# A gated recurrence and a gated feed-forward block on one core: transposes of q and k moved from the DMA crossbar to TensorE, and slab groups 4, 4, 4, 4, 4, 2, 2 with a new order

## The chip, the cores and the metric

The kernel runs on one core of a Trainium2 chip. The metric is the device time of one execution in microseconds (us); lower is better. An execution's time holds the span (first to last instruction) and a little more around it.

The engines are PE (TensorE, matrix products; PEld are its weight loads), DVE (VectorE), ACT (ScalarE, which has to load a table when it changes between some functions), POOL (GpSimd) and SP (SyncE, which here only issues DMAs). Each engine works through its own queue in the order in which instructions were put there. 16 DMA engines move the data.

## The reference

```python
B, H, S, D = 4, 8, 768, 48
mag = sqrt(a_re**2 + a_im**2)
scale = minimum(mag, 0.999) / (mag + 1e-6)
a_re_n, a_im_n = a_re * scale, a_im * scale
for t in range(S):                       # per batch and head; state is D x D, complex
    new_re = ar * S_re - ai * S_im       # ar, ai: row t of a_re_n, a_im_n
    new_im = ar * S_im + ai * S_re
    S_re, S_im = new_re + outer(k[t], v[t]), new_im
    y[t] = q[t] @ S_re
x = y, heads joined: (B * S, 384)
gate = sigmoid(x @ w_gate)               # 384 -> 1536
out = (gate * (x @ w_val)) @ w_out       # 1536 -> 384, fp32, (3072, 384)
```

## The kernel before

The sequence is cut into 6 chunks of 128 rows. A *slab* is one chunk of one batch with all heads, 128 rows x 384 columns; there are 24, in the order chunk 0 of batches 0 to 3, chunk 1 of batches 0 to 3, and so on. Slab m belongs to batch m % 4. `SIZES` puts neighbouring slabs into groups; some steps are done once for a group (logarithms, the exponential of them, the arctangent), the others once for a slab or a pair.

The recurrence of a chunk is made parallel by writing the decay as a magnitude and an angle and summing both over the rows.

- `lr`, `la` load the two parts of a for a slab, `sq` and `add` make the squared magnitude, `lna`, `lnm`, `inv`, `r`, `atan` turn it into log magnitude and angle for the whole group. `lh`, `ll`, `th`, `tl` split them into two fp16 parts; `SPLIT` says in which groups.
- `cl` sums the log magnitudes over the rows by a matmul with a triangular matrix (fp32 in the first four slabs, two fp16 matmuls in the others), `ee` takes the exponentials exp(+) and exp(-), `qke` multiplies q and k with them (`lk`, `lq`, `lv` load k, q, v; `v16` makes v fp16).
- `ct` sums the angles, `r16` and `nid` bring them into one turn, `cr` carries the last row to the next chunk, `ab` and `cs` make cosine and sine. `qs` multiplies q and k by both and writes the *slot* of the slab: for each head 128 columns (cosine and sine parts, with a gap of zeros), for q and for k.
- q and k must then lie with the rows of the slab along the free axis. Slabs in `CROSSED` (6 to 23) do it by DMA: `xk` and `xq` are one transposing DMA each (line 871), issued on SP's queue, from the slot into a tile `qkT`. The others (0 to 5) do it on PE: `tp` transposes the eight 128x128 blocks of four heads into one PSUM bank (lines 892 and 893), and `qkT` copies the bank to the tile (the helper of lines 517 to 521, on DVE or ACT). There are two such halves in a slab.
- `sc` makes the scores k x q, four heads to a bank, `mst` applies the triangular mask on DVE. `kv` and `P` add the chunk's k x v to the batch's state; `u` and `x16` decay the state by the factor of the chunk and make it fp16. `y` adds masked scores x v and q x state; `y16`, `xp`, `xt` scale and transpose the result for the feed-forward block.
- The feed-forward block works on pairs of slabs. `pg` and `pv` (line 1043) are the gate and value products, 72 steps of each, 6 matmuls to a step, `tanh` on ACT gives the gate, `p` on DVE multiplies (line 1061), `po` (line 1082) multiplies by w_out in three steps for each slab, `ot` copies the bank out and `st` stores it. `wg`, `wv`, `wo` load the weights on POOL's queue.

All steps are recorded in a plan, and the order in which they are put into the queues is written out by hand: `TIMES` has a due time for each step of each kind, and steps are issued in the order of these times. So a step's place in every queue follows from its due time, SP's loads, stores and transposing DMAs too. `HOME` says by a letter for each slab or pair which engine does a step (v DVE, a ACT, g POOL). `SLOTS` gives the buffer of each tile, and of each PSUM bank under "ps" (8 banks). `WARM` puts dummy matmuls of 128 columns ahead of a step on PE (line 1131). Table loads for ACT are put where the order needs them (line 1125).

Of the kernel before, what the change touches and what calls it, by code (L numbers as in the profile page):

```python
# [27 lines left out]
CROSSED = range(6, 24)  # L28
# [3 lines left out]
SPLIT = range(2, 8)  # L32
MSTP = ()
HOME = {
    "sq": "vagvaaggaagagagaaggagggg",
    "add": "vvvvgggggggggggggggggggg",
    "lh": "gvggggvggggg",
    "r": "vvgggggggggg",
    "v16": "vavagaggggagggggagavaaga",
    "qke": "vvvggggvggggggggggggvggg",  # L40
    "th": "aagvaagvgaav",
    "ab": "vvavvavaavaaaaaaaaaavaaa",
    "qkT": "vavavvvvavvvvvvvvvvvvvvvvvvvvvvvvvvvvvvvvvvvvvvv",
    "P": "vava",
    "u": "ggggggvggggggggggvgg",
    "x16": "ggaavgaggggvggag",
    "y16": "avvvaavvavavvvavaaavaaaa",
    "xt": "vvvvvvavvvvvavvavvvvvaav",
    "ot": "vvvvvaaavvvvavvaaavvaaavv",
}  # L50
SIZES = [2, 2, 4, 4, 4, 4, 2, 2]
TIMES = {
    "wg": [
        27.89, 36.02, 27.27],
    "wv": [
        31.35, 38.17, 36.03],
    "wo": [
        53.47, 54.3, 65.03],
    "lr": [
        0.75, 2.68, 7.03, 7.06, 24.34, 27.88, 25.83, 26.32, 45.89, 58.15,  # L60
        53.31, 52.18, 71.46, 92.9, 87.25, 85.33, 106.38, 121.07, 118.57,
        112.93, 170.37, 176.96, 133.38, 160.02],
    "la": [
        2.22, 1.85, 10.78, 7.07, 24.5, 26.36, 25.84, 27.87, 48.76, 56.39,
        53.93, 53.32, 75.86, 92.85, 87.77, 85.34, 111.4, 121.08, 121.86,
        118.56, 176.57, 178.21, 153.22, 134.91],
    "sq": [
        7.04, 7.02, 11.86, 9.9, 24.95, 29.54, 26.34, 29.5, 49.21, 58.89,
        56.85, 62.71, 83.72, 96.51, 92.96, 86.01, 112.9, 129.56, 128.24,
        118.61, 180.83, 185.55, 167.29, 170.36],  # L70
    "add": [
        7.05, 7.9, 13.4, 13.88, 26.35, 38.15, 28.5, 38.12, 53.3, 65, 62,
        65.86, 87.2, 96.54, 96.47, 92.92, 121.81, 129.58, 128.25, 129.55,
        184.23, 185.57, 169.56, 170.39],
    "lna": [
        9.92, 14.99, 33.31, 67.86, 98.47, 139.01, 185.56, 171.42],
    "lh": [
        8.54, 14.47, 40.53, 42.65, 69.29, 75.89, 102.61, 103.34, 136.22,
        141.84, 185.59, 172.91],
    "lnm": [  # L80
        11.87, 15.39, 38.16, 66.46, 100.65, 132.15, 185.58, 170.4],
    "inv": [
        9.93, 16.37, 36.01, 70.07, 103.36, 139.02, 186.18, 172.85],
    "r": [
        10.77, 19.16, 40.52, 39.65, 73.59, 75.88, 108.19, 107.9, 142.65,
        142.64, 189.11, 173.82],
    "cl": [
        14.97, 14.96, 17.84, 16.27, 45.44, 42.85, 47.17, 46.54, 70.89, 76.95,
        80.11, 77.54, 104.14, 104.52, 114.2, 116.75, 138.97, 140.17, 148.32,
        149.93, 187.16, 186.78, 181.01, 173.23],  # L90
    "ee": [
        16.91, 14.98, 18.49, 17.83, 47.18, 44.65, 48.42, 47.56, 72.96, 79.27,
        86.25, 79.29, 106.53, 106.39, 114.78, 117.62, 140.01, 141.81, 149.19,
        152.85, 189.76, 189.77, 182.5, 173.81],
    "scr": [
        35.3, 38.13, 41.19, 37.26, 52.64, 53.49, 54.34, 53.48, 87.94, 92.86,
        95.76, 92.91, 118.58, 111.43, 121.83, 124.54, 153.21, 155.22, 160.22,
        160.21, 195.89, 195.1, 187.57, 187.58],
    "rbt": [
        46.92, 48.74, 55.48, 96.46, 126.03, 161.47, 198.36, 188.29],  # L100
    "arr": [
        50.09, 50.04, 55.92, 98.24, 127.86, 161.92, 205.03, 188.88],
    "lk": [
        16.93, 15.41, 15.42, 17.85, 30.76, 49.23, 53.94, 66.48, 75.91, 85.35,
        94.86, 88.08, 112.25, 92.84, 112.27, 118.55, 125.19, 156.21, 161.95,
        146.39, 185.54, 190.51, 161.93, 181.02],
    "lq": [
        16.94, 16.28, 16.95, 21.91, 41.18, 50.73, 62.72, 69.68, 79.24, 92.87,
        95.78, 88.09, 112.26, 104.92, 122.21, 118.59, 155.19, 156.9, 161.96,
        146.4, 190.31, 197.73, 161.94, 190.12],  # L110
    "lv": [
        15.4, 29.55, 9.91, 26.79, 30.86, 50.74, 71.28, 66.47, 52.19, 92.94,
        76.96, 95.79, 133.17, 121.82, 125.2, 146.64, 160.01, 154.52, 171.41,
        166.24, 140.93, 180.62, 192.37, 195.11],
    "v16": [
        15.89, 30.3, 14.95, 27.29, 45.52, 60.69, 71.29, 84.58, 87.19, 101.96,
        114.07, 118.91, 136.26, 130.58, 142.92, 147.37, 164.44, 155.21,
        178.63, 169.53, 167.28, 202.72, 198.62, 205.05],
    "qke": [
        17.82, 16.36, 20.04, 24.35, 48.73, 53.28, 67.87, 71.45, 84.59, 93.48,  # L120
        96.49, 92.93, 112.96, 108.55, 134.93, 121.8, 157.53, 160.03, 167.43,
        157.52, 209.72, 205.09, 191.58, 190.32],
    "atan": [
        14.48, 21.92, 40.57, 75.9, 108.2, 143.28, 191.6, 176.95],
    "ct": [
        15.44, 15.43, 22.66, 24.05, 48.2, 49.65, 58.14, 59.2, 83.81, 87.93,
        91.11, 87.21, 116.85, 121.09, 130.19, 122.59, 151.79, 158.27, 164.99,
        155.16, 205.89, 202.2, 191.28, 189.92],
    "r16": [
        15.45, 18.69, 23.57, 25.71, 49.24, 50.7, 58.9, 59.78, 84.57, 89.07,  # L130
        91.94, 87.95, 117.61, 121.2, 132.12, 123.7, 152.84, 159.36, 165.57,
        156.87, 207.37, 204.03, 192.35, 190.49],
    "nid": [
        16.92, 19.28, 24.33, 26.3, 49.49, 52.17, 59.3, 60.37, 85.16, 89.47,
        92.89, 88.87, 118.54, 121.4, 132.33, 124.35, 153.03, 160, 166.46,
        157.5, 208.97, 205.07, 192.97, 191.11],
    "cr": [
        20.92, 23.58, 25.85, 28.76, 50.72, 53.37, 62.74, 64.56, 87.18, 91,
        95.81, 89.85, 119.29, 122.19, 134.27, 126.29, 156.88, 161.48, 167.96,
        157.86],  # L140
    "ab": [
        17.28, 20.91, 26.31, 26.78, 52.62, 53.29, 60.7, 63.2, 87.24, 91.46,
        95.8, 89.46, 118.9, 122.61, 134.26, 126.3, 155.17, 162.17, 167.97,
        158.26, 209.12, 205.47, 195.76, 192.33],
    "cs": [
        21, 23.59, 26.51, 30.73, 52.63, 54.33, 65.04, 65.87, 88.07, 92.06,
        98.25, 91.47, 121.01, 124.52, 134.92, 126.94, 156.89, 162.18, 170.33,
        160.19, 209.71, 205.48, 195.77, 192.34],
    "qs": [
        21.9, 24.04, 29.56, 33.52, 54.31, 56.84, 67.89, 72.97, 89.48, 94.21,  # L150
        98.26, 92.95, 122.6, 125.18, 136.25, 128.26, 157.55, 163.7, 175.58,
        160.2, 210.61, 207.38, 198.38, 192.88],
    "tp": [
        24.94, 24.49, 26.86, 25.82, 30.88, 33.51, 34.4, 34.25, 56.38, 61.19,
        63.19, 59.9],
    "qkT": [
        26.18, 26.33, 27.86, 28.51, 34.86, 34.87, 38.11, 38.14, 59.65, 61.99,
        63.91, 61.2],
    "sc": [
        30.87, 26.8, 29.51, 30.31, 36, 35.29, 39.63, 38.75, 63.38, 62.7,  # L160
        64.55, 65.43, 76.51, 76.73, 80.49, 79.88, 99.76, 98.23, 103.88,
        103.37, 108.76, 108.54, 110.29, 105.52, 133.14, 130.57, 133.37,
        132.11, 144.9, 144.91, 141.57, 146.38, 167.92, 166.23, 170.32, 170.09,
        182.04, 182.27, 179.73, 179.08, 219.4, 218.3, 218.53, 215.46, 205.46,
        204.01, 202.19, 202.47],
    "mst": [
        30.89, 27.26, 31.34, 30.74, 37.25, 35.55, 40.05, 39.66, 64.58, 63.18,
        64.99, 65.85, 79.26, 77.55, 82.04, 82.03, 102, 99.99, 104.53, 103.57,
        110.54, 110.53, 114.09, 106.37, 133.57, 132.13, 134.9, 133.19, 145.74,
        145.73, 144.93, 148.33, 168.49, 167.42, 171.45, 170.52, 184.25,  # L170
        183.56, 182.51, 181.03, 220.93, 221.67, 220.95, 217.02, 205.91,
        204.43, 204.02, 204.04],
    "kv": [
        30.75, 40.06, 77.33, 35.62, 84.19, 72.09, 98.02, 90.24, 111.38,
        111.17, 121.02, 125.17, 144.87, 141.37, 152.83, 166.03, 180.81,
        171.19, 180.6, 186.17],
    "P": [
        39.64, 45.46, 79.28, 40.54, 87.17, 75.87, 101.65, 90.99, 112.95,
        112.94, 121.1, 127.85, 144.94, 142.63, 153.44, 168.15, 183.57, 186.38,
        181.05, 192.36],  # L180
    "y": [
        31.46, 33.3, 37.89, 42.66, 67.91, 67.88, 87.23, 85.97, 102.59, 105.07,
        116.74, 121.03, 136.85, 137.26, 146.6, 148.7, 171.4, 171.84, 186.37,
        183.14, 221.99, 221.25, 207.36, 205.1],
    "y16": [
        34.24, 34.88, 38.76, 42.68, 69.67, 69.27, 88.11, 86.71, 103.55,
        105.77, 116.76, 121.13, 138.98, 139, 148.73, 149.96, 172.01, 172.45,
        187.59, 187.81, 222.6, 222.41, 207.97, 205.88],
    "xp": [
# [201 lines left out]
def kernel(  # L391
# [165 lines left out]

    for g, n in enumerate(SIZES):
        m0 = FIRST[g]
# [602 lines left out]
```

## Time and profile before

| | us |
|---|---|
| median of 3 runs (lowest, highest) | 247.29 (247.19, 247.33) |
| the profiled execution's own time | 246.99 |
| its span | 244.9 |
| PE busy | 215.4 |
| DVE busy | 206.3 |
| ACT busy | 198.6 |
| POOL busy | 145.9 |

The profile is one execution with the time of every instruction. Busy times are sums over the whole span, and stages differ in what limits them; matmuls are pipelined, so that a busy PE is not PE at its peak. A line of a group gives line, engine, operation, output and inputs, shape and count, then the busy time in us and the mean of one instruction in ns, then the idle time just before them and what ended it. Of the DMA queues, SP's moved 37.80 MB in 166800 packets (loads, stores and transposing DMAs), the one of POOL 3.57 MB.

### The profile page before, as it was taken

The page shows a single profiled execution, that of the slowest core. Times are in us where ns is not written, and L with a number is a line of the kernel's source. Part 1 is how long each engine was busy: PE and PEld are TensorE (multiplying, and loading weights), DVE is VectorE, ACT ScalarE, POOL GpSimd, SP SyncE. Part 2 cuts the span into 40 slices and gives each one's busy share as a digit, 9 for nine tenths or more (in the row PEclk, how much of TensorE's full clock was granted, in tenths as well). Part 3 has the DMA queues.
Part 4 walks back from the last instruction along what each step waited for, and adds up shares of the span by engine and source line. Part 5 has one row for each costly group of instructions (what it writes and reads, how often), then busy time and mean ns, then how long its engine had stood idle before and what let it go on. Part 6 is the DMA issues. An engine that isn't in the chain of part 4 may idle for free.

```text
span 244.9 us, 6068 instructions
## 1 busy us (share of the span) xinstructions
PE 215.4 (88%) x2319; PEld 168.5 (69%) x2319; DVE 206.3 (84%) x317; ACT 198.6 (81%) x326; POOL 145.9 (60%) x138
## 2 busy tenths in 40 slices
PE   0376899959787997999999999999999999999993
PEld 0234688738556865778867778877788777788981
DVE  4589999999888999999999979989887977988250
ACT  2899899948599989999989999996899995542341
POOL 2305977895567899758659986499776683100000
PEclk9999999999999999999999999999999999999999
DMA  7999999999999999999999998979999569073011
GB/s 144 215 218 212 197 183 192 177 191 175 177 180 137 202 244 186 196 177 219 197 192 205 195 212 172 220 165 178 196 191 205 131 136 197 35 141 98 3 64 66
DMA packets 171004, 41.75 MB, mean 170 GB/s; under 512 B 163916, under 2 KB 170976, under 8 KB 170976
## 3 DMA queue, kind: packets, MB, share of 16 engines
q1 hardware_dynamic: 166800, 37.80, 78.3%
q0 software_dynamic: 4176, 3.57, 9.6%
q8 instruction: 18, 0.29, 0.5%
q14 instruction: 10, 0.08, 0.1%
HBM read 30.67 MB, written 4.72 MB: 145 GB/s over the span
## 4 chain that ended last, share of the span: by engine, by line
PE 50%; DVE 15%; ACT 13%; SPq 8%; DMA 8%; issue 4%; DVEq 0%; ACTq 0%
PE banks L1043 25%; PE banks L1082 15%; SPq L552 7%; DMA qk<-in_q_dram 5%; DVE a L768 3%; DVE slot L851 3%; PE banks L911 2%; DVE p L1061 2%; ACT g L1054 2%; DMA qk<-in_k_dram 2%; PE banks L783 2%; DMA a<-in_a_im_dram 1%; DVE qk L728 1%; DVE r L798 1%; ACT lm L604 1%
## 5 line engine op out<-in xcount | busy, mean ns | idle before, releaser
L1061 DVE SCALAR_TENSOR_TENSOR p<-g,banks 128x512 f16<-128x512 f16 x72 | 47.7, 681 | 12.5 <-ACT g L1054 7.4
L1043 PE MATMUL banks<-xt,wg 128*128 128x256 f16 x432 | 56.0, 273 | 0.7 <-DVE xt L521 0.4
L1043 PE MATMUL banks<-xt,wv 128*128 128x256 f16 x432 | 56.2, 273 | 0.0
L1082 PE MATMUL banks<-wo,p 128*128 128x384 f16 (+1 forms) x300 | 55.5, 320 | 0.5 <-ACT g L1054 0.3
L1054 ACT ACTIVATE g<-banks 128x512 f16<-128x512 f32 x72 | 41.2, 601 | 16.8 <-PE banks L1043 11.6
L1043 PEld LDWEIGHTS <-wg 128*128 128x128 f16 x432 | 40.9, 98 | 7.8 <-issue 1.5
L1043 PEld LDWEIGHTS <-wv 128*128 128x128 f16 x432 | 41.4, 98 | 6.8 <-issue 0.5
L728 POOL TENSOR_TENSOR qk<-qk,ee 128x768 f32<-128x768 f32 x19 | 35.3, 1863 | 14.5 <-ACT cr L815 6.8
L851 DVE TENSOR_TENSOR slot<-qk,banks 128x1536 f16<-128x1536 f32 x24 | 41.8, 1745 | 1.7 <-issue 1.3
L1082 PEld LDWEIGHTS <-p 128*128 128x128 f16 x300 | 27.7, 97 | 14.6 <-issue 1.6
L1125 ACT ACT_TABLE_LOAD x28 | 35.9, 1283 | 0.5
L926 DVE TENSOR_TENSOR mst<-banks,msk_t 128x512 f16<-128x512 f32 x48 | 31.9, 685 | 3.4 <-PE banks L911 2.9
L647 POOL TENSOR_TENSOR a<-a 128x768 f32<-128x768 f32 x10 | 18.7, 1884 | 10.7 <-ACT a L641 8.6
L591 POOL TENSOR_TENSOR lm<-sq 128x384 f32<-128x384 f32 x20 | 21.2, 1064 | 4.2 <-ACT sq L583 3.8
L585 POOL TENSOR_TENSOR sq<-a 128x768 f32<-128x768 f32 x12 | 18.2, 1513 | 6.2 <-DMA a<-in_a_im_dram 4.3
L911 PEld LDWEIGHTS <-qkT 128*128 128x128 f16 x192 | 13.2, 97 | 3.2 <-DVE qkT L521 1.1
L940 POOL TENSOR_TENSOR state<-state,arr 128x384 f32<-128x384 f32 x15 | 12.5, 837 | 4.2 <-DVE arr L697 3.4
L583 ACT ACTIVATE sq<-a 128x768 f32<-128x768 f32 x10 | 8.6, 856 | 7.9 <-DMA a<-in_a_re_dram 7.8
L658 PE MATMUL banks<-lm,wl_t 128*128 128x384 f32 x8 | 4.6, 700 | 10.9 <-ACT lm L604 10.9
L768 DVE SCALAR_TENSOR_TENSOR a<-a 128x768 f16<-128x768 f32 x10 | 13.8, 1409 | 0.0
L798 DVE TENSOR_SCALAR r<-banks 128x384 f16<-128x384 f32 x24 | 13.2, 549 | 0.6 <-PE banks L783 0.4
L815 ACT ACTIVATE cr<-banks 32x384 f32<-32x384 f32 x20 | 9.7, 484 | 4.7 <-PE banks L805 4.0
(93 smaller groups left out, 411.8 us busy)
## 6 DMA issues: line engine op xcount, KB each, us to landing
a<-in_a_re_dram SPq DMA_DIRECT2D x24, 192.0 KB
a<-in_a_im_dram SPq DMA_DIRECT2D x24, 192.0 KB
v<-in_v_dram SPq DMA_DIRECT2D x24, 192.0 KB
qk<-in_k_dram SPq DMA_DIRECT2D x24, 192.0 KB
qk<-in_q_dram SPq DMA_DIRECT2D x24, 192.0 KB
out_dram<-ot SPq DMA_DIRECT2D x23, 192.0 KB
wg<-in_moe_w_gate_dram POOLq DMA_DIRECT2D x3, 384.0 KB, 7.7
wv<-in_moe_w_val_dram POOLq DMA_DIRECT2D x3, 384.0 KB, 10.6
```

Source lines behind the costliest of these rows:

```text
L585: on.tensor_tensor(out=T[SQ], in0=T[A][:, :, s], in1=T[A][:, :, s], op=ALU.mult)
L591: home("add", m).tensor_tensor(out=T[LM][:, s], in0=T[SQ][:, 0], in1=T[SQ][:, 1], op=ALU.add)
L647: home("r", w).tensor_tensor(out=T[A][:, 1, i:j], in0=T[A][:, 1, i:j], in1=T[A][:, 0, i:j], op=ALU.mult)
L728: home("qke", m).tensor_tensor(out=T[QK], in0=T[QK], in1=T[EE], op=ALU.mult)
L768: nc.vector.scalar_tensor_tensor(out=turns(T)[:, i:j, 1], in0=T[A][:, 1, i:j], scalar=1.0 / TWO_PI, op0=ALU.mult, in1=turns(T)[:, i:j, 0], ...
L851: nc.vector.tensor_tensor(out=T[SL].rearrange("p i h (r x) -> p r i h x", r=2)[:, :, :, :, 0:D], in0=T[QK].rearrange("p i (h d) -> p i h d ...
L926: nc.vector.tensor_tensor(out=T[MS][:, :n_], in0=T[SC], in1=msk_t.unsqueeze(1).broadcast_to([L, n_, L]), op=ALU.mult)
L1043: nc.tensor.matmul(T[ACC][:, r], wt[:, j, f0:f0 + 128], T[XT][:, :, j], start=(j == 0), stop=(j == 2))
L1054: nc.scalar.activation(out=T[G16], in_=T[PG], func=FT.Tanh, scale=0.5)
L1061: nc.vector.scalar_tensor_tensor(out=T[PT][:, 2 * fp:2 * fp + 2], in0=T[G16], scalar=1.0, op0=ALU.add, in1=T[PV], op1=ALU.mult)
L1082: nc.tensor.matmul(T[PO][:, :wd], T[PT][:, fb, s0:s0 + L], wo16[:, fb, c0:c0 + wd], start=(fb == 0), stop=(fb == NFB - 1))
L1125: nc.scalar.preload_act_table_set(SETS[key[1]])
```

## The change

`CROSSED` becomes empty: the 18 slabs that used the transposing DMA get the two PE halves with their copies. `SIZES` has one group of four where it had two groups of two, so there are 7 groups, and `SPLIT` moves by one so that the same slabs (4 to 23) are split. `HOME` is new, and with it the engine of many copies and products. `WARM` has 39 dummies in 6 places where it had 131 in 16. All due times in `TIMES` are new, and so are the buffers in `SLOTS`. The functions themselves are not changed.

```diff
-CROSSED = range(6, 24)
+CROSSED = ()
...
-SPLIT = range(2, 8)
+SPLIT = range(1, 7)
...
 HOME = {
-    "sq": "vagvaaggaagagagaaggagggg",
-    "add": "vvvvgggggggggggggggggggg",
-    "lh": "gvggggvggggg",
-    "r": "vvgggggggggg",
-    "v16": "vavagaggggagggggagavaaga",
-    "qke": "vvvggggvggggggggggggvggg",
-    "th": "aagvaagvgaav",
-    "ab": "vvavvavaavaaaaaaaaaavaaa",
-    "qkT": "vavavvvvavvvvvvvvvvvvvvvvvvvvvvvvvvvvvvvvvvvvvvv",
-    "P": "vava",
-    "u": "ggggggvggggggggggvgg",
-    "x16": "ggaavgaggggvggag",
-    "y16": "avvvaavvavavvvavaaavaaaa",
-    "xt": "vvvvvvavvvvvavvavvvvvaav",
-    "ot": "vvvvvaaavvvvavvaaavvaaavv",
+    "sq": "vaaavvvaaagaggaagggaagaa",
+    "add": "vvvgvvggggggggvggggggggg",
+    "lh": "gggggggggggg",
+    "r": "vvgggggggvvg",
+    "v16": "vagggaggggaaggggggagggaa",
+    "qke": "ggvggggggggggggggggggggg",
+    "th": "aagaggaggggg",
+    "ab": "vvaaaaaaaaavaaaaaaaavava",
+    "qkT": "vvvvvavavvvvvvvavvvvvavvavavvvvvvvavvvvvaaavaaav",
+    "P": "aava",
+    "u": "ggggggggggggggvvggvv",
+    "x16": "gavggggggagggagg",
+    "y16": "vvvvvvvvaaaaaaaaavavvaaa",
+    "xt": "vvvvvvvaaaaaavvvvvvvavav",
+    "ot": "aavavaavavaaavaavaavaavaa",
 }
-SIZES = [2, 2, 4, 4, 4, 4, 2, 2]
+SIZES = [4, 4, 4, 4, 4, 2, 2]
 TIMES = {
...
     "lr": [
-        0.75, 2.68, 7.03, 7.06, 24.34, 27.88, 25.83, 26.32, 45.89, 58.15,
-        53.31, 52.18, 71.46, 92.9, 87.25, 85.33, 106.38, 121.07, 118.57,
-        112.93, 170.37, 176.96, 133.38, 160.02],
+        0.75, 2.22, 8.01, 9.14, 9.95, 16.21, 21.88, 27.67, 54.09, 61.82,
+        55.21, 68.04, 78.46, 78.5, 78.47, 85.51, 114.73, 134.98, 114.74,
+        120.84, 178.69, 188.92, 133.43, 143.03],
     "la": [
-        2.22, 1.85, 10.78, 7.07, 24.5, 26.36, 25.84, 27.87, 48.76, 56.39,
-        53.93, 53.32, 75.86, 92.85, 87.77, 85.34, 111.4, 121.08, 121.86,
-        118.56, 176.57, 178.21, 153.22, 134.91],
+        6.07, 1.85, 8.02, 8.49, 17.48, 16.2, 21.24, 23.26, 58.24, 60.68,
+        58.21, 61.83, 79.32, 87.46, 78.48, 85, 117.33, 126.57, 116.29, 123.02,
+        180.26, 183.23, 153.95, 150.14],
     "lk": [
-        16.93, 15.41, 15.42, 17.85, 30.76, 49.23, 53.94, 66.48, 75.91, 85.35,
-        94.86, 88.08, 112.25, 92.84, 112.27, 118.55, 125.19, 156.21, 161.95,
-        146.39, 185.54, 190.51, 161.93, 181.02],
+        21.9, 23.27, 16.53, 25, 35, 55.04, 48.74, 36.71, 83.01, 80.95, 94.19,
+        46.03, 98.46, 92.34, 123, 117.34, 117.35, 159.5, 167.13, 167.12,
+        204.58, 130.84, 138.83, 195.46],
     "lq": [
-        16.94, 16.28, 16.95, 21.91, 41.18, 50.73, 62.72, 69.68, 79.24, 92.87,
-        95.78, 88.09, 112.26, 104.92, 122.21, 118.59, 155.19, 156.9, 161.96,
-        146.4, 190.31, 197.73, 161.94, 190.12],
+        21.92, 23.28, 21.91, 34.96, 39.21, 58.22, 51.6, 54.45, 87.49, 85.53,
+        110.58, 90.76, 122.96, 124.67, 127.43, 122.97, 117.74, 161.89, 176.99,
+        167.14, 207.77, 206.46, 204.57, 196.11],
...
-    "xk": [
-        75.93, 79.44, 96.52, 102.6, 108.18, 99.11, 126.31, 126.39, 141.85,
-        140.02, 164.45, 167.94, 178.22, 175.93, 215.7, 213.52, 203.36, 202.18],
-    "xq": [
-        75.92, 79.43, 96.53, 102.62, 107.24, 105.51, 126.04, 127.84, 144.86,
-        140.57, 164.49, 167.95, 180.61, 165, 217.04, 214.81, 203.37, 202.14],
...
 WARM = {
-    ('cl', 3): 5,
-    ('ct', 2): 43,
-    ('sc', 0, 1): 3,
-    ('sc', 1, 0): 3,
-    ('sc', 1, 1): 3,
-    ('sc', 0, 0): 11,
-    ('y', 1): 29,
-    ('kv', 3): 4,
-    ('kv', 1): 3,
-    ('pv', 0, 0): 5,
-    ('pv', 1, 4): 3,
-    ('pg', 1, 3): 5,
-    ('ct', 7): 3,
-    ('y', 5): 1,
-    ('cl', 8): 5,
-    ('pv', 2, 5): 5,
+    ('cl', 3): 3,
+    ('y', 0): 23,
+    ('pg', 0, 4): 1,
+    ('kv', 0): 3,
+    ('sc', 6, 0): 4,
+    ('pg', 2, 5): 5,
 }
```

Left out are the other rows of `TIMES` (the row `tp` grows from 12 to 48 entries, as does `qkT`) and `SLOTS`, in which "ps" grows from 353 to 388 allotments.

## The prediction, made before the changed kernel ran

> **What bounds the kernel now.** I read the page first, then the stretches, then the chain of waits, then the groups of instructions by line and shape, then SP's own queue. The profiled execution took 246.99 us, 0.30 below the median of 247.29; its span is 244.88 and 2.11 lie around it. The sums below are made against 246.99.
>
> ```profile
> PE 215.4 (88%) x2319; PEld 168.5 (69%) x2319; DVE 206.3 (84%) x317; ACT 198.6 (81%) x326; POOL 145.9 (60%) x138
> PEclk9999999999999999999999999999999999999999
> DMA  7999999999999999999999998979999569073011
> ```
>
> The stretches give PE, PEld, DVE, ACT, POOL busy time, clock and DMA share:
>
> ```profile
> 0.00:37.33 37.33, 21.67 (x248) 16.09 (x249) 30.21 (x51) 30.55 (x45) 18.03 (x25) 1.00 1.05 195
> 60.00:80.00 20.00, 16.15 (x181) 12.00 (x179) 16.83 (x23) 16.63 (x26) 13.82 (x14) 1.00 1.07 167
> 80.00:100.00 20.00, 17.69 (x190) 13.21 (x189) 19.52 (x29) 18.65 (x35) 17.52 (x15) 1.00 1.05 210
> 100.00:120.00 20.00, 19.92 (x235) 16.38 (x232) 19.57 (x34) 19.67 (x27) 14.12 (x14) 1.00 1.09 192
> 120.00:220.00 100.00, 99.57 (x1062) 77.75 (x1060) 87.64 (x134) 86.19 (x149) 65.06 (x61) 1.00 0.85 175
> ```
>
> The reader sees two regimes. From 120 us on PE never stops; before it PE, DVE, ACT and the DMA engines take turns. The chain of waits says the same; its pieces give start, length, what:
>
> ```profile
> 13.85 3.54 DMA qk<-in_q_dram
> 56.03 7.89 DMA qk<-in_q_dram
> 80.42 1.33 SPq L871
> 82.41 3.52 DMA a<-in_a_im_dram
> 115.54 4.25 DMA qk<-in_k_dram
> 139.00 0.45 PE banks L911 x8
> 229.18 7.86 PE banks L1043 x72
> 237.04 3.91 PE banks L1082 x24
> ```
>
> A busy PE is not yet a full one, so I count by spacing, start to start. A gate or value matmul of 256 columns takes 7.86/72 = 109 ns, one of 384 columns 3.91/24 = 163 ns, one of 128 columns 0.45/8 = 56 ns; the 48-column ones step by 25 ns in the chain. In 120 to 220 us the groups count 423 of 256 columns (46.1 us), 180 output and 55 other matmuls of 384 (38.3), 116 of 128 (6.5), 272 of 48 (6.8) and some 0.8 of tiny ones: 98.5 of 100 us. That stretch is full of real work. The same count over 37.33 to 120 gives 67.0 us of 82.7 (342 at 109 ns, 106 at 163, 128 at 56, 181 at 25, 0.8 tiny), so PE loses 15.7 there, 30 dummies of 56 ns (1.7) included. Up to the first gate matmul at 37.33 it gives 16.5 (fp32 matmuls some 10), so 20.8 are lost, 101 dummies (5.6) included. After the last output matmul at 240.95 come one eviction and the store, 3.9 us.
>
> **The change part by part.** *Crossbar out, TensorE in.* The rows with prices:
>
> ```profile
> L871 SPq DMA_TRANSPOSE qkT<-slot x36: 1231/1285/2492, 72.8 to 218.8; - x36
> L893 PE MATMUL banks<-idn_t,slot 128*128 128x128 f16 x48 | 6.3, 219 | 0.0
> L521 DVE COPY qkT<-banks 128x1024 f16<-128x1024 f16 x9 | 6.0, 682 | 0.9 <-PE banks L893 0.9
> L519 ACT ACTIVATE qkT<-banks 128x1024 f16<-128x1024 f16 x3 | 3.1, 1017 | 0.0
> 25.28 0.22 PE L892 MATMUL banks<-idn_t,slot 128*128 128x128 f16 x1
> 25.34 0.22 PE L893 MATMUL banks<-idn_t,slot 128*128 128x128 f16 x1
> ```
>
> All 36 DMA transposes go (slabs 6 to 23, two each); 18 slabs x 16 = 288 PE transposes come, 8 to a PSUM bank, and 36 more evictions. Each transpose lasts 219 ns, but the next starts 56 ns later (25.28 to 25.34): 288 x 55.6 ns = 16.0 us. SP's queue in order of time shows 12 of the 36 issued before 120 us and 24 after. So 192 PE transposes, **10.7 us**, fall where PE has 98.5 of 100 us taken: nothing covers them. The other 96, 5.3 us, fall where PE loses 15.7; cover exists there, but it is time in which PE waits for DVE and ACT, which get the evictions too. Bounds 0 and 5.3; I take **5.3**, as DVE and ACT are at 98% in the last 20 us of that front.
>
> A rule weighed here: the Trainium skill, "TensorE: Matmul & The Clock Gate", Part 4, gives some 275 ns for a PE transpose inside a kernel and says that transposes do not engage the full clock. By it the 288 would cost an estimated 79 us and the time would be about 325. The trace's spacing of 56 ns speaks against it here, and I go by the trace.
>
> *Evictions and new homes.* By the HOME letters, each with the mean of its own row, the copies to qkT add 26 x 0.682 on DVE and 10 x 1.017 on ACT. Squares, adds, products with ee, output and other copies change hands. DVE ends 7 us up in all (206 to 213): the evictions' 17.7 less mostly 5.3 for products and 3.8 for output copies. ACT ends about 13 up (199 to 211): 10.2 of evictions, 3.5 output copies, 2.6 squares, less two table loads (28 due before, 26 by the new order, 1.283 each) and 0.8 for merging the first groups. POOL rises by 2 of 148. Behind 120 us both have 12 to 14 us free in 100, so I price this at 0 there. In front it is what forbids the cover above. If they bind there by themselves, a third of ACT's 13 is 4.2 us more.
>
> *What each hand-over may add.* PE waits 0.9 us for an eviction ahead of transposes and 0.5 ahead of scores over today's 12 halves, 0.12 each. For the 24 late halves that is 2.8 us at most; PE has other steps queued, so I take 0. One more PSUM bank is needed per half (388 allotments on 8 banks against 353); no row shows a wait that is only for a bank, so it stays inside that 2.8.
>
> *What the DMA queue gets back.* 36 x 1.285 = 46 us of SP issuing and 36 x 256 KB = 9.4 of 41.75 MB go. Behind 120 us PE waits for no transfer, so this is worth 0. Before 72.8 us no transpose ran, so the 7.89 us wait at 56 us stays. What can shrink is 3.52 + 4.25 of landing waits and 1.33 of issue on the chain: bounds 0 and 9.1. Between 72.8 and 120 the 12 transposes are 3.1 of some 9.2 MB, a third: a third of 7.8 and the whole 1.3 give **-3.9**.
>
> *The start.* With 2 + 2 slabs the first group's matmul starts at 10.03 us, the second's at 15.83; as one group of four all wait for the fourth slab, up to 5.8 us. SP's queue decides more closely. Before, the last k or q that slabs 0 and 1 need is the 15th load, landing at 13.85 + 3.54 = 17.39. In the new order six loads of a for slabs 4 to 6 come earlier, a seventh (slab 7's) too, and slab 1's q is the 22nd. At 195 GB/s a load of 192 KB drains in 1.0 us: 24.4. Its product with ee moves from DVE to POOL (2 us): 26.4, against 24.70 for the second slot product now. So 1.7 to 5.8 later, and below zero not, as both slabs are needed for the first pair. DVE, 4 us lighter there, wins some back, so 0 stays in the range. I take **+3.0**.
>
> *Dummies.* 131 become 39. 101 of them stand before 37.33 us, where PE has 15 us idle besides, so their 5.1 us are worth 0. The granted clock reads full in every slice and no row shows a slow matmul, so I can't price a colder start. As a far end, chosen and not read, I let the 6.5 us of fp16 work ahead of the first gate matmul (16.5 - 10) take twice as long, mostly beside DVE work, and take 0.
>
> **Sum:** 246.99 + 10.7 + 5.3 - 3.9 + 3.0 = 262.1 us.
>
> **The rivals.**
> - *The front was held by the DMA engines* (the other side). Their share is about 1 up to 140 us and the chain has DMA in it. If the relief gave back all 15.7 us that PE loses between 37.33 and 120, and the two table loads 2.6 more, the time would be 246.99 + 16.0 - 18.3 = 244.7. It decides only where more than 16.0 us come back, and the 20.8 lost at the start hold no transpose. DVE and ACT at 98% in 100 to 120 speak against it. Chance 0.04.
> - *Early transposes are covered, the start slips little:* only the late stretch counts, 246.99 + 10.7 - 3.9 + 1 = about 255. For it: PE's 15.7 free us. Chance 0.14.
> - *ACT and DVE become the bound:* the front's 4.2, the hand-overs' 2.8 and no relief (3.9): 262.1 + 10.9 = about 273, or half of it, 267.5. For it: ACT's +13. Chance 0.16.
> - *The change doesn't do what it says:* no slab is left in CROSSED, so each takes the PE branch; no chance.
>
> **How the numbers follow.** The forecast has 0.66, the others 0.14, 0.16 and 0.04. The range 252 to 269 takes in the second rival and the nearer half of the third, and leaves out the first. About 0.2%, 0.5 us, is what a measurement of this kernel can tell from no change. Only the first rival reaches down to it: faster 0.03, same 0.01, slower 0.96.
>
> **What would show it.** Right: 384 matmuls on the two transpose lines at some 56 ns spacing, 48 evictions, no DMA transpose; PE full from about 125 us to the end, 4 us of tail; first gate matmul near 40 us; 27 table loads with the one of the preamble; DMA share below 0.9 behind 75 us. Wrong: PE with several us of idle behind 130 us (the hand-overs bind), a transpose spacing above 60 ns, or a first gate matmul before 37 us together with PE full from 100 us on (the DMA rival).

## The result, and the profile after

The changed kernel takes 261.26 us (median of 4, 260.02 to 263.29) against 247.31 of the kernel before (median of 4, 247.19 to 248.78). The ratio is 1.0558, 95% interval 1.0476 to 1.0639: 14 us slower. The forecast was 262.1, range 252 to 269. The profiled execution took 260.66 us, with a span of 258.9. The ratios, here and below, leave out executions more than 1.5% above the fastest of their kernel; the medians hold all.

The page of the changed kernel, the same three lines as before (busy time; granted clock and DMA share in 40 slices):

```profile
PE 226.8 (88%) x2511; PEld 180.6 (70%) x2511; DVE 212.2 (82%) x325; ACT 210.1 (81%) x341; POOL 149.2 (58%) x144
PEclk9999799999999999999999999999999999999999
DMA  7999999999789842999278015674514240000211
```

Its stretches (PE, PEld, DVE, ACT, POOL busy; clock, DMA share, GB/s), cut at the first gate matmul and at 80, 120 and 254.9 us:

```profile
0.00:42.86 42.86, 20.21 (x192) 13.96 (x193) 31.17 (x54) 34.76 (x45) 23.04 (x29) 0.96 1.04 191
42.86:80.00 37.14, 33.75 (x392) 27.77 (x392) 33.44 (x53) 35.00 (x58) 29.60 (x29) 1.00 0.97 176
80.00:120.00 40.00, 37.69 (x419) 28.96 (x418) 38.64 (x56) 38.19 (x65) 32.16 (x28) 1.00 0.77 160
120.00:254.90 134.90, 134.85 (x1512) 109.88 (x1510) 108.97 (x165) 101.39 (x175) 64.36 (x61) 1.00 0.35 80
```

PE is again busy without a break from 120 us on, now for 135 us in place of 121. The DMA engines are no longer loaded there: over 120 to 220 us their share is 0.43, where it was 0.85. The groups that are new or grown:

```profile
L885 PE MATMUL banks<-idn_t,slot 128*128 128x128 f16 x192 | 26.8, 223 | 3.8 <-DVE slot L844 3.1 <-ACT banks L820 0.7
L886 PE MATMUL banks<-idn_t,slot 128*128 128x128 f16 x192 | 26.7, 223 | 0.0
L514 DVE COPY qkT<-banks 128x1024 f16<-128x1024 f16 x35 | 23.6, 685 | 2.7 <-PE banks L886 2.4
L512 ACT ACTIVATE qkT<-banks 128x1024 f16<-128x1024 f16 x13 | 13.1, 1033 | 2.4 <-PE banks L886 2.3
```

384 transposes, 48 copies, at nearly the durations read before (219 ns; 682 and 1017 ns for the copies). The chain of waits by engine, and the piece of it that the forecast of the start rests on:

```profile
PE 55%; ACT 14%; DVE 9%; SPq 7%; issue 6%; POOL 5%; DMA 1%; ACTq 0%; POOLq 0%; DVEq 0%
```

```profile
20.54 3.31 DMA qk<-in_q_dram
```

DMA is down from 8% of the chain to 1%. The last load that the first pair needs lands at 23.85 us, where the forecast had 24.4.

The best summary is a ledger of PE, made with the forecast's spacings (109, 163, 56 and 25 ns; fp32 steps of the first slabs 0.72 and 0.49 us, output halves 82 ns). *Lost* is all time that is not such work, dummies included. Stretches: to the first gate matmul, from there to 120 us, from there to the end of the span.

| us | span | first gate matmul | work, all | lost to it | lost to 120 | lost behind |
|---|---|---|---|---|---|---|
| before | 244.9 | 37.33 | 202.8 | 20.9 | 15.6 | 5.7 |
| after | 258.9 | 42.86 | 218.4 | 25.2 | 10.5 | 4.8 |
| before, transposes left out | 244.7 | 38.23 | 202.7 | 21.9 | 14.1 | 6.0 |
| after, transposes left out | 253.8 | 42.67 | 202.4 | 24.9 | 15.7 | 10.7 |
| after, late transposes left out | 259.7 | 42.60 | 207.9 | 24.8 | 12.4 | 14.6 |
| after, late transposes twice | 272.1 | 45.51 | 229.1 | 27.9 | 9.2 | 5.9 |
| after, early transposes twice | 262.7 | 44.59 | 223.9 | 26.9 | 6.6 | 5.3 |

From before to after: 15.6 more work, 4.3 more lost at the start, 5.1 less in front, 0.9 less behind, 13.9 of the 14.0 us between the spans. The experiments tell what this ledger may be read for, and what not.

### The profile page after: what moved, and what is told of

The parts are those of the page before. It is cut to its first block, busy times and chain, and to the rows that moved or that the text cites. A ratio compares the mean times of both kernels' runs of the same rounds, so it can differ in the third digit from the quotient of the medians.

```text
span 258.9 us, 6440 instructions
## 1 busy us (share of the span) xinstructions
PE 226.8 (88%) x2511; PEld 180.6 (70%) x2511; DVE 212.2 (82%) x325; ACT 210.1 (81%) x341; POOL 149.2 (58%) x144
## 4 chain that ended last, share of the span: by engine, by line
PE 55%; ACT 14%; DVE 9%; SPq 7%; issue 6%; POOL 5%; DMA 1%; ACTq 0%; POOLq 0%; DVEq 0%
PE banks L1036 25%; PE banks L1075 15%; SPq L545 7%; PE banks L904 3%; ACT L1118 3%; PE banks L885 2%; PE banks L886 2%; POOL qk L721 2%; ACT g L1047 2%; DVE mst L919 2%; PE banks L776 1%; DVE qkT L514 1%; DVE p L1054 1%; DVE lh L624 1%; DMA qk<-in_q_dram 1%
## 5 line engine op out<-in xcount | busy, mean ns | idle before, releaser
L1036 PE MATMUL banks<-xt,wv 128*128 128x256 f16 x432 | 57.0, 272 | 0.2 <-DVE slot L844 0.2
L721 POOL TENSOR_TENSOR qk<-qk,ee 128x768 f32<-128x768 f32 x23 | 45.3, 1975 | 18.8 <-ACT ee L665 9.3
L1036 PEld LDWEIGHTS <-wg 128*128 128x128 f16 x432 | 41.5, 98 | 8.0 <-issue 1.3
L885 PE MATMUL banks<-idn_t,slot 128*128 128x128 f16 x192 | 26.8, 223 | 3.8 <-DVE slot L844 3.1
L886 PE MATMUL banks<-idn_t,slot 128*128 128x128 f16 x192 | 26.7, 223 | 0.0
L514 DVE COPY qkT<-banks 128x1024 f16<-128x1024 f16 x35 | 23.6, 685 | 2.7 <-PE banks L886 2.4
L885 PEld LDWEIGHTS <-slot 128*128 128x128 f16 x192 | 18.9, 99 | 5.7 <-DVE slot L844 4.9
L584 POOL TENSOR_TENSOR lm<-sq 128x384 f32<-128x384 f32 x18 | 17.9, 1005 | 5.7 <-ACT sq L576 5.4
L904 PE MATMUL banks<-qkT 128*128 128x128 f16 x192 | 17.9, 225 | 2.4 <-DVE y L507 0.7
L886 PEld LDWEIGHTS <-slot 128*128 128x128 f16 x192 | 19.1, 100 | 1.1 <-issue 0.3
L904 PEld LDWEIGHTS <-qkT 128*128 128x128 f16 x192 | 13.8, 101 | 5.3 <-DVE qkT L514 2.3
L576 ACT ACTIVATE sq<-a 128x768 f32<-128x768 f32 x13 | 11.1, 855 | 7.0 <-DMA a<-in_a_re_dram 4.8
```

The costliest lines, as they stand in the source:

```text
L514: on.tensor_copy(out=dst, in_=src)
L721: home("qke", m).tensor_tensor(out=T[QK], in0=T[QK], in1=T[EE], op=ALU.mult)
L885: nc.tensor.transpose(tp[:, 4 + i], T[SL][:, 1, h], idn_t)
L886: nc.tensor.transpose(tp[:, i], T[SL][:, 0, h], idn_t)
L904: nc.tensor.matmul(sc[:, 4 * hf * both + i], kt, qt, start=True, stop=True)
L1036: nc.tensor.matmul(T[ACC][:, r], wt[:, j, f0:f0 + 128], T[XT][:, :, j], start=(j == 0), stop=(j == 2))
```

## The experiments

In each, the ratio is to runs of the kernel before, made beside it on the same chip; a difference to the changed kernel is the difference of ratios times 247.3 us. The intervals of the ratios reach 0.4 to 0.8% (1 to 2 us) to each side, so that differences of 1 or 2 us stay open; the forecast had reckoned with 0.5 us. Line numbers in the lines shown are those of the experiment's own kernel.

**1. Late transposes twice.**

```diff
-                    def e(T, TP=TP, SL=SL, hf=hf):
+                    def e(T, TP=TP, SL=SL, hf=hf, again=2 if m >= 12 else 1):
...
-                        for i in range(4):
+                        for i in list(range(4)) * again:
```

> The changed kernel with the PE transposes of slabs 12 to 23 made twice into the same bank (192 more, nothing else). Theory 1, PE is full from 120 us on and a transpose costs its spacing of 56 ns there: 192 x 55.6 ns = 10.7 us on top of 261.3, so 271.9 (260.7 to 272.5 covers run to run). Theory 2, the hand-overs (evictions, ACT, DVE) set the pace late and PE has room: under 4 us more, so below 265.

Measured: 274.14 us, ratio 1.1089 (1.1005 to 1.1173), 13.1 more than the changed kernel. In the ledger the work rises by 10.7, as priced; 2.7 more were lost before the first gate matmul, which came at 45.5 us in this execution; no added transpose stands there, and the last section shows what did it. Adding to PE late costs its full spacing: PE is full there.

**2. Early transposes twice.** The same edit with `6 <= m < 12`.

> The changed kernel with the PE transposes of slabs 6 to 11 made twice (96 more). The forecast's price, no cover before 120 us: 5.3 us more, 266.6. The rival, early transposes are covered by time that PE loses anyway: 0 to 1.5 us more, below 262.8.

Measured: 264.05 us, 1.0623 (1.0550 to 1.0696), 1.6 more, and within the intervals of both. The work rises by 5.5, the time lost between the first gate matmul and 120 us falls from 10.5 to 6.6. So added early transposes are in good part covered; the two intervals together leave the 1.6 open by 2.7 us to each side, and the 5.3 of no cover lie outside. The forecast had taken them as uncovered.

**3. New order, crossbar back.** The due times of the DMAs in words:

```diff
-CROSSED = ()
+CROSSED = range(6, 24)
...
-    t_qkT = kind("qkT", 6, [L, 8, L], F16)
+    t_qkT = kind("qkT", 8, [L, 8, L], F16)
...
+    "xk": [  # the due time of the slab's first "tp", which goes
+    "xq": [  # the same
```

> The changed kernel with slabs 6 to 23 back on the transposing DMA, each pair of them issued where the first PE half stood; groups, homes and the other order as changed, 8 qkT buffers in place of 6. Theory 1 undoes 10.7 + 5.3 - 3.9: 261.3 - 12.1 = 249.2, the rest over 247.3 being the start. Rival, the new order and groups cost by themselves: it stays above 255. Rival, the DMA engines held the front: it rises above 261.

Measured: 307.88 us, 1.2403 (1.2330 to 1.2476). By its size it falls under both rivals (above 255, above 261), but neither had named what its profile shows. Three of its waits (us in total, times, longest); L688 is the transposing DMA, L668 the slot product, L545 the product with ee, L728 the scores:

```profile
SPq L688 <- DVE slot L668: 37.8, 8, 9.1
```

```profile
POOL qk L545 <- DMA qk<-in_q_dram: 30.2, 7, 13.7
```

```profile
PE banks L728 <- DMA qkT<-slot: 11.0, 9, 3.8
```

A transposing DMA on SP's queue waits for its slot product, and every load queued behind it waits too: POOL then stands 30.2 us for q (7.4 in the changed kernel), PE loses 104 us in all. In the changed kernel no step on SP reads a slot, and SP's waits for the slot products are 6.6 us (loads that need a buffer); its loads were placed with no transposing DMA among them. Putting the DMAs back costs far more here than the transposes that they save. The run says nothing on the price of the crossbar itself.

**4. Old order, transposes on PE.** The due times in words:

```diff
-CROSSED = range(6, 24)
+CROSSED = ()
...
-    "qkT": "vavavvvvavvvvvvvvvvvvvvvvvvvvvvvvvvvvvvvvvvvvvvv",
+    "qkT": "vavavvvvavvvvvvavvvvvavvavavvvvvvvavvvvvaaavaaav",
...
+    "tp": the two halves at the due time of the slab's DMAs and 0.45 later
+    "qkT": 0.7 and 1.4 later; "sc" not before 1.5 and 2.2 later
```

> The kernel before with no slab on the transposing DMA: the PE halves of slabs 6 to 23 and their copies stand where the DMAs stood, the scores 1.5 us later; copies shared between DVE and ACT as in the changed kernel, all other homes and the groups as before. Theory 1: 247.3 + 10.7 + 5.3 - 3.9 = 259.4, and up to 4 more because DVE and ACT were not relieved for the copies. Rival, the DMA engines held the front: 248 or less.

Measured: 293.31 us, 1.1833 (1.1771 to 1.1896): 34 above the 259.4 that theory 1 expected, and 30 above the 263.4 that it allowed at most. Its waits; L718 is the second transpose line, L346 and L344 are the copies on DVE and ACT:

```profile
DVE qkT L346 <- PE banks L718: 12.2, 11, 4.4
ACT qkT L344 <- PE banks L718: 9.7, 8, 3.0
POOL qk L553 <- ACT ee L497: 18.3, 4, 7.5
```

A copy put into DVE's or ACT's queue where its transposes are not yet through PE's queue holds all behind it: 21.9 us for these two rows alone. PE's work is 218.5, as in the changed kernel, but 71.7 us are lost against 40.5. In the changed kernel the same two waits are 2.4 and 2.3 us in all: its order has places for the copies, the old one has not.

**5. and 6. No transposes at all, in both orders.** Transposes and copies of slabs 6 to 23 are left out, scores and state products read one constant tile.

```diff
-            QT = [t_qkT(m, 0), t_qkT(m, 1)]
+            QT = [] if by_dma else [t_qkT(m, 0), t_qkT(m, 1)]
...
-                            kt, qt = (T[x][:, 4 * hf + i] for x in QT)
+                            kt, qt = qkc[:, 4 + i], qkc[:, i]
...
+    qkc = const.tile([L, 8, L], F16, name="qkc")
+    nc.gpsimd.memset(qkc, 0.0)
```

> The kernel before with the 36 transposing DMAs of slabs 6 to 23 left out: scores and state products of these slabs read a constant tile in place of transposed q and k. Order, homes, groups and dummies as before. Theory 1: behind 120 us PE is full and waits for no DMA, so only the front's relief shows, 3.9 us at most 9.1: 243.4 (238 to 247.3). Rival, the DMA engines and SP's queue hold the front: below 238.

> The changed kernel with the PE transposes of slabs 6 to 23 and their copies left out in the same way (constant tile). Theory 1: late 10.7 us go in full, of the early 5.3 between half and all: 261.3 - 10.7 - 2.7 to 5.3 = 245.3 to 247.9; more than the transposes' 16.0 can go only if the copies bound DVE and ACT: then below 245. Against the other kernel without transposes (243.4) this leaves some 2 to 4 us for the start and the new order.

Measured: in the old order 247.14 us, 0.9999 (0.9962 to 1.0036); in the new order 256.53, 1.0390 (1.0348 to 1.0432). The DMA row of the first of the two (slices of 6.1 us) against that of before shows what went:

```profile
DMA  7999999999996996207982518981626560001011
```

The DMA engines are idle for much of 90 to 220 us, and the time does not move: the crossbar cost the kernel before nothing, within the 0.9 us of the interval. And without any transpose the new order is still 3.9%, 9.6 us, slower than the old one, with the same work on PE (202.4 against 202.7); 4.2 us of the 13.8 between the two kernels go with the transposes and their copies. In the ledger the new order then loses 5.2 more in front than with them and 5.9 more behind.

**7. Late transposes left out.** The same edit, for slabs 12 to 23 only.

> The changed kernel with the PE transposes and copies of slabs 12 to 23 left out (scores and state products of these slabs read a constant tile), those of slabs 0 to 11 kept. Theory on record, PE full late: 261.3 - 10.7 = 250.6. New theory, from leaving out all 288 (4.7 us back of 16.0): the order's own gaps open as soon as the transposes go, so 3 to 5 us back, 256 to 258.

Measured: 261.72 us, 1.0514 (1.0461 to 1.0567), 1.1 less than the changed kernel and inside the intervals of both: next to nothing for 10.5 us of work taken from a PE that was full. The stretch from 140 to 160 us, first of the changed kernel, then of this one:

```profile
140.00:160.00 20.00, 20.00 (x235) 17.20 (x233) 17.81 (x28) 18.82 (x31) 14.14 (x15) 1.00 0.21 45
```

```profile
140.00:160.00 20.00, 17.76 (x189) 15.00 (x188) 13.89 (x21) 18.20 (x29) 15.20 (x16) 0.91 0.26 56
```

PE has gaps as soon as the transposes go. Its granted clock is 0.91 there as well, so that some of what came free went into slower steps, an estimated 1.8 us in this stretch (0.09 of 20 us). The chain of this kernel runs into the stretch through a load of a, POOL's square and POOL's decay of the state:

```profile
132.65 4.88 DMA a<-in_a_re_dram
139.09 1.47 POOL sq L402
140.56 1.57 POOL state L748 x2
```

So the feed (loads in their places in SP's queue, then POOL, ACT and DVE in theirs) delivers slabs hardly faster than PE takes them. Two bounds lie almost on one another: adding to PE costs all of it, taking from PE gives almost nothing. Run 6 differs from this one only in the early transposes and their copies, and is 3.1 us faster (1.0390 against 1.0514): taken away early, transposes give back more than late ones, and more than the 1.6 that another 96 cost, but again less than 5.3.

**8. First loads forward.**

```diff
-    "lk": [21.9, 23.27, 16.53,
+    "lk": [9.2, 9.4, 9.6,
...
-    "lq": [21.92, 23.28, 21.91,
+    "lq": [9.3, 9.5, 9.7,
```

> The changed kernel with the loads of q and k of slabs 0, 1 and 2 moved ahead of the loads of a for slabs 4 to 6 in SP's queue (from places 13 to 22 to places 9 to 14). The start term on record was 3.0 us, read from this queue. If q's place sets the start: first gate matmul from 42.9 us to about 40, time down by 1 to 3 us, 258.3 to 260.3. If DVE and ACT set it: no change (within 0.5 us).

Measured: 269.50 us, 1.0920 (1.0875 to 1.0964), 9.0 more, and the first gate matmul at 49.6 us. Neither expectation. DVE's queue in this kernel (L400 squares, L406 adds), and POOL's products with ee beside it:

```profile
19.14 0.96 DVE L400 TENSOR_TENSOR sq<-a 128x768 f32<-128x768 f32 x1 [3.19 <-DMA a<-in_a_re_dram]
20.51 0.96 DVE L400 TENSOR_TENSOR sq<-a 128x768 f32<-128x768 f32 x1 [0.41 <-DMA a<-in_a_im_dram]
21.51 4.13 DVE L406 TENSOR_TENSOR lm<-sq 128x384 f32<-128x384 f32 x2
```

```profile
21.30 3.92 POOL L543 TENSOR_TENSOR qk<-qk,ee 128x768 f32<-128x768 f32 x2 [8.24 <-ACT ee L487]
```

The squares of slabs 4 to 6 stand in DVE's queue ahead of the slot products of slabs 0 to 3. With their loads six places later DVE waits at them: the last of the three squares ends at 26.76 us, 6.4 later than in the changed kernel, the first slot product starts at 32.65, and the first gate matmul comes 6.7 later. So the run measures what those loads of a hold up when they come late. Whether the place of q's load sets the start in the changed kernel, it does not tell.

**9. More dummies before the first transposes.**

```diff
 WARM = {
+    ('tp', 0, 0): 30,
...
+                if key[0] == "tp":
+                    nc.tensor.transpose(tiles[st[2][0]][:, 0], zero, idn_t)
+                    continue
```

> The changed kernel with 30 more dummy transposes of zeros on PE just ahead of the first transposes, at 26 to 27.7 us, where PE waits. In its profile 128-column steps between 29.5 and 33 us come 107 ns apart in place of 56 and the granted clock is lower there. If the dummies keep the clock up: spacing 56 ns there, first gate matmul about 1 to 2 us earlier, time down by 0.5 to 2 us. If DVE and ACT pace that stretch, or the dummies do nothing for the clock: no change (within 0.5 us).

Measured: 261.19 us, 1.0570 (1.0523 to 1.0617), no change that the intervals show; first gate matmul at 44.5. The slow stretch was not taken away but moved: the added transposes of zeros ran at the slow spacing themselves, 3.15 us for 30, and held the first real ones until 30.22 (27.77 in the changed kernel):

```profile
27.24 3.15 PE L1126 MATMUL banks<-idn_t,zero 128*128 128x128 f16 x30 [1.55 <-DVE slot L845]
30.28 0.22 PE L887 MATMUL banks<-idn_t,slot 128*128 128x128 f16 x1
30.34 0.22 PE L886 MATMUL banks<-idn_t,slot 128*128 128x128 f16 x1
```

**10. First group of four alone.**

```diff
-SIZES = [2, 2, 4, 4, 4, 4, 2, 2]
+SIZES = [4, 4, 4, 4, 4, 2, 2]
...
-SPLIT = range(2, 8)
+SPLIT = range(1, 7)
```

> The kernel before with its first two groups of two joined to one of four and nothing else changed; 15 due times of slabs 0 to 3 are pushed back just behind what they now wait for, six buffers' turns follow. New theory: of the 14 us between the two kernels 9.4 belong to the new order without any transpose, and its first gate matmul is 4 to 5 us later; if the group of four does that, the first gate matmul here moves from 37.3 us to about 42 and the time rises by 3 to 5 us, to 250 to 252. Rival, DVE and ACT pace the start and take the group in: within 1 us of before.

Measured: 257.61 us, 1.0338 (1.0295 to 1.0381), 8.4 more; first gate matmul at 47.6. That is later than in the changed kernel, which has the same group and its first gate matmul at 42.9. SP's queue shows a part of why. Its longest wait in the first 60 us (us, times, longest) is 11.7 us at one load, for a buffer of v that ACT has still to read:

```profile
SPq L379 <- ACT v L339: 11.7, 1, 11.7
```

So a group of four delays the start in these queues; how much of the changed kernel's delay is its work, this run does not tell.

**11. New homes alone.** The `HOME` letters of the changed kernel but for qkT, in the kernel before.

> The kernel before with the HOME letters of the changed kernel (all but those of qkT), its order, groups and crossbar as before. If the new homes cost by themselves (18 of 19 products with ee stay on POOL and 4 more go there, 7 output copies go to ACT): 2 to 5 us slower. If they are neutral and only the order counts: within 1 us of before.

Measured: 277.10 us, 1.1108 (1.1057 to 1.1159), 27 more. PE's work is the same (202.5), 73.2 are lost against 42.1. SP's stores wait 20.4 us for output copies on ACT (5.3 in the kernel before), its transposing DMAs 15.5 us for slot products (9.1 before). Homes and order belong together: a step that moves to another engine without a place made for it there can hold that engine's queue, and SP's with it.

**12. y by DMA**, an attempt at a version faster than both: `YCROSSED = range(10, 20)` in the kernel before, the DMA at the due time of the scaled y.

```diff
-YCROSSED = ()
+YCROSSED = range(10, 20)
```

> The kernel before with the transposes of y of slabs 10 to 19 (3 on PE and one copy each) made by a transposing DMA on SP's queue, issued where the scaled y is due. PE gives up 30 x 56 ns = 1.7 us where it is full, and 10 copies of 0.35 to 0.49 us go: 1 to 2 us faster than before if PE's work is all that counts. Rival, the DMA waits at the head of SP's queue for y and holds the loads behind it: slower by 2 us or more.

Measured: 274.29 us, 1.1004 (1.0959 to 1.1050), 25 more. The rival holds in its sign, and at ten times its size. Its waits agree with it: the DMAs of y (L832) stand at the head of SP's queue, their three longest waits for DVE and ACT 18.3 us in all, POOL waits 20.1 us for loads of q (4.5 in the kernel before) and 18.7 for loads of v, and PE 7.0 for the transposed y. How much of the 25 each of them makes was not told apart.

## Why the prediction was right, and where its steps were not

The time was right within 1 us, and the ledger shows the sum of the right size. In part that was luck: two wrong terms, the third and the fourth below, cancelled. Step by step:

- **A transpose at 56 ns, 16.0 us for 288.** Right: 15.6 more work in the ledger, and run 1 adds 10.7 for 192. The page "TensorE: Matmul & The Clock Gate" (Part 4) of the Trainium skill gives some 275 ns for a transpose. From that the forecast had estimated 325 us, and rightly did not go by it: 223 ns is how long one lasts here, 56 ns how far the next one is.
- **10.7 late, with nothing to cover them.** Right as a cost of adding (run 1), and wrong if read as what there is to win: run 7 took them out and got 1.1 back. The forecast had found one bound and not asked for the next one beneath.
- **5.3 early, no cover.** Wrong step. Run 2: another 96 cost 1.6, and the time lost in front fell by 3.9; taking the 96 away gave 3.1 (runs 6 and 7). The DVE and ACT shares of 98% were read as forbidding the cover.
- **-3.9 of relief for the DMA queue.** Wrong step. Run 5: without the crossbar 0.9999. The landing waits on the chain were real, but something else was due almost as late: without the transposing DMAs the chain has no transfer between 63.5 and 124.3 us, DVE, ACT and PE fill it, and the time is the same. These two errors cancelled: together they gave 1.4, where runs 2 and 5 measured 1.6 and nothing.
- **+3.0 at the start.** The size was near: 4.3 more lost and the first gate matmul 5.5 us later, where 1.7 to 5.8 had been given. The reason was one of two. q's load landed as read (at 23.85, 24.4 forecast) and POOL's product with it ended at 25.81, but ACT, busy almost without a break from 13.05 us on with the group of four and the table loads, ended the sines and cosines of the first slab at 25.86 (L833, 0.47 us from 25.39). The first slot product started right behind both:

```profile
24.01 1.80 POOL qk L721
```

```profile
25.95 3.53 DVE L844 TENSOR_TENSOR slot<-qk,banks 128x1536 f16<-128x1536 f32 x2 [0.28 <-POOL qk L721]
```

An earlier q alone could therefore have gained next to nothing, and runs 8 and 10, in which other steps moved too, do not part the two. The first transposes came 2.5 us later than before (27.77 for 25.28); the other 3.0 arose between them and the first gate matmul, which the sum for the start did not hold.

- **Homes and table loads.** The busy sums came out as worked (DVE 212.2 for 213, ACT 210.1 for 211, POOL 149.2 for 148; 26 table loads, where the list of signs had 27); behind 120 us PE hardly ever stood (134.85 of 134.9 us busy), so they cost nothing beside the transposes. What they do in queues not made for them is run 11.
- **Dummies at 0.** Not contradicted: 30 dummies put in at one place did not move the time (run 9), the other places were not tried. (The 5.1 us is the price of the 92 that go, not of the 101.) The clock that the forecast could not price did drop. The rivals: the transposing DMAs did not hold the front (run 5), and ACT and DVE were no bound behind 120 us as long as the transposes were there.

What is shown and what stays open: with the transposes out the new order keeps 9.6 of the 13.8 us, so the larger part of the loss does not come back by taking the transposes and their copies away. Part of that is the start (3.0 more lost than in the old order without transposes), 4.7 are gaps behind 120 us, which in the changed kernel the transposes fill. Which of the group of four, the homes and the due times makes the feed that slow was not told apart: the homes alone, put into queues made for the other kernel, cost twice the whole change and the group more than half of it, and the due times alone were not run.

## What to carry to other kernels

A ledger of the bounding engine, counts times spacing, can predict a sum and still not say what would come back: price a load that is added by the full engine, but before promising a gain from taking work away, look for the next bound just beneath. In queues worked in order, an operation's home, its place and what its neighbours wait for are one thing: undoing a single part of a fitted order measures the misfit (8 to 46 us here, each against the kernel that was edited), not the part. To price a resource, leave its work out where the order stays as it is (0.9999 for the crossbar), do not swap it for another.

## What the runs showed of the hardware

The granted clock fell in the start of the changed kernel. There 26 dummies stand ahead of the first gate matmul in place of 101, and 23 of them only at 34.21 us. The first 16 transposes came 56 ns apart; from 29.6 us on they came 107 ns apart, and from 33.0 us 55 again:

```profile
29.72 0.31 PE L885 MATMUL banks<-idn_t,slot 128*128 128x128 f16 x1
29.83 0.31 PE L886 MATMUL banks<-idn_t,slot 128*128 128x128 f16 x1
33.08 0.22 PE L886 MATMUL banks<-idn_t,slot 128*128 128x128 f16 x1
33.13 0.22 PE L885 MATMUL banks<-idn_t,slot 128*128 128x128 f16 x1
```

It is the slice with the 7 in the clock row. The same page of the skill, Part 1, says that PE falls to half its clock after an idle window of some 3.4 us and needs as long of work to rise again. The rows agree in the factor (107 to 55) and in the length of the slow stretch (29.6 to 33.0 us), and run 9, whose 30 added transposes ran slow for 3.15 us and the next ones at full speed, agrees too. An idle window of that length they do not show: ahead of the drop PE waited 1.42, 1.55 and 0.71 us, with short work between.

Kernels whose start is the same had their first gate matmul anywhere from 42.6 to 45.5 us. In the two that were late, runs 2 and 1 (44.6 and 45.5), ACT waited 1.0 and 1.8 us for a load of v, for which the others did not wait, PE then stood, and the steps behind ran slow again: eight score matmuls took 1.01 us in place of 0.61.

DVE's fp32 operations were stretched where they began beside one of POOL's. The two adds of run 8 took 4.13 us together beside POOL's two products (the same two took 1.03 in the changed kernel, with POOL idle), and in the kernel before one product on DVE took 2.57 us, while POOL ran its own, against 0.95 where POOL was idle. A product moved from DVE to POOL so can slow what stays on DVE as well; the forecast had not priced that, and DVE's busy sum, 212.2 for 213, shows no cost of it in all.
